# An attention and gating kernel whose vector work is dealt out anew over the engines, and whose head and batch ends are ordered anew

## The chip, the cores and the metric

The kernel runs on one core of a Trainium2 chip. The metric is the device time of one execution in microseconds (us). The engines are PE (matmul), DVE (vector), ACT (scalar functions), POOL and SP; each works through its own instructions in order. PE writes to PSUM, from where DVE and ACT read; POOL reads and writes SBUF alone. POOL and SP also issue DMAs, in the order of their other instructions.

## The reference

Four batches of q, k and v, each 6336 x 256. For each batch a 256 x 256 attention matrix over the channels is made from column-normed q and k; v times this matrix is x, and a gate with two 256 x 256 weights follows.

```python
qn = q / (np.linalg.norm(q, axis=1, keepdims=True) + 1e-06)
kn = k / (np.linalg.norm(k, axis=1, keepdims=True) + 1e-06)
s = kn.transpose(0, 2, 1) @ qn / tau
a = softmax(s)                       # over the last axis
x = (v @ a).reshape(25344, 256)
H = np.maximum(x @ w_h, 0.0)
T = 1.0 / (1.0 + np.exp(-(x @ w_t + b_t)))
out = T * H + (1.0 - T) * x
```

## The kernel before

**Tiles.** A batch is 49 tiles of 128 rows and a tail of 64. Tiles come in six chunks (8, 8, 8, 8, 8, 9 tiles); q, k and v are loaded chunk by chunk with a cast to f16 (`load_chunk`, L74), all by DMAs that POOL issues. There are 9 chunk buffers each for q and k, 7 for v. The output leaves by chunks too, in three buffers, by DMAs that SP issues (L392).

**Gram work.** `stage1(b, i)` (L160 to L162) is one gram unit: for one tile of q and k six matmuls add k'q, k'k and q'q into `sg` (two PSUM banks). A batch has 50 units (49 tiles and the tail).

**Chain.** `chain(b)` makes the batch's matrix from `sg` in five steps. `norms` takes the diagonals on DVE (L181), the square root on ACT (L191), and 1/norm on DVE; `bcast` spreads the column factors by a matmul with ones (L212) into PSUM; `soft` multiplies on DVE (L220), takes Exp on ACT (L226) and scales on DVE (L240) into `mr`; `trans` transposes `mr` on PE (L255) with a copy on DVE (L257); `fold` multiplies it with both gate weights (L265), and the copies to f16 (L272 on ACT, L273 on DVE) complete `mr` = [a, a w_h, a w_t].

**Slots.** A batch has 25 slots (`npair`), each two tiles of v. Slot i of batch b issues, in this order: `main(b, i)`, with four matmuls of 512 columns into `xh` = [x, x w_h] (L324; two buffers of two banks) and, into `tt` (one bank), the bias b_t by a matmul of 512 columns (L331) and x w_t (L335); then `pending`, the last slot's `finish`; then `elementwise(b, i)`; then `transposes` of the v tiles two slots ahead (L303 into `vtps`, one PSUM bank, copied by DVE in L306); then `issue_loads`, which issues the loads whose buffers are free by then; then, while there is a next batch, two or three of its gram units, 50 over 18 slots, and after them one step of its chain per slot.

**Elementwise.** With hh = relu(x w_h) on ACT (L351), uu = 1 - T by a Sigmoid with scale -1 on ACT (L354) and dd = hh - x on DVE (L359), the product dd = uu * dd runs on POOL (L367). `finish` writes o = hh - dd on DVE (L384) and, at the end of a chunk, its store.

**Order.** The order is written out by hand: each engine takes its instructions in the order in which this code issues them. Before the slots all of batch 0's gram units, its loads, its chain and two `transposes` are issued. A buffer that is used again waits for its last reader.

## Time and profile before

| | us |
|---|---|
| median of three runs | 379.46 (378.46 to 380.11) |
| profiled execution | 382.07 |
| span of the profiled execution, first to last instruction | 380.3 |
| PE busy in it | 294.3 (77%) |
| DVE, ACT, POOL busy | 186.9, 147.3, 170.7 |
| chain of waits that ended last, by engine | PE 46%, DMA 17%, DVE 13%, POOL 12% of the span |

The profile is of one execution, 0.7% above the median. Its shares are means over stages that differ, so the stretches in the next section but one are read one by one: loads and gram of batch 0, the slots of batches 0 to 2 with the next batch's gram units in the first 18 and its chain in the last 7, and batch 3 without gram work. "Idle before, releaser" in a row is how long the engine stood idle before that instruction and whose end let it go.

### The profile page before, as it was taken

The numbers are of one execution on the slowest core, as the hardware profiler recorded it, in microseconds if no ns is written. First come the engines' busy times: TensorE is split into PE (matmuls) and PEld (weight loads), VectorE is DVE, ScalarE is ACT, GpSimd is POOL, SyncE is SP. The second block draws the span as 40 slices with busy tenths as digits, with TensorE's granted clock in tenths as the row PEclk, the third lists the DMA queues.
The fourth block names the chain that finished last, engine by engine and source line by source line (L and its number), as shares of the span: only waits on it lengthen the run. The fifth ranks groups of instructions, "written<-read, shape, count | busy, mean of one in ns | idle before, by whom it ended". The sixth has DMA issues, their size and how long they took to land.

```text
span 380.3 us, 6361 instructions
## 1 busy us (share of the span) xinstructions
PE 294.3 (77%) x2540; PEld 204.1 (54%) x2540; DVE 186.9 (49%) x394; ACT 147.3 (39%) x251; POOL 170.7 (45%) x189
## 2 busy tenths in 40 slices
PE   0937639089999679999996889999977876767650
PEld 0836516067777445777774457777744444434320
DVE  0000132056555757556557566555665765656551
ACT  1000033114333674344336753344466644444430
POOL 6242212355466525654665254444442545444441
PEclk9997967779999989999999799999998999999995
DMA  7999999999999993999999925566335032222113
GB/s 138 209 162 214 210 214 214 214 213 268 258 242 248 266 266 66 259 240 210 215 237 231 243 41 175 162 167 165 69 110 164 0 133 110 110 112 97 49 77 132
DMA packets 15821, 65.68 MB, mean 173 GB/s; under 512 B 1712, under 2 KB 3504, under 8 KB 12720
## 3 DMA queue, kind: packets, MB, share of 16 engines
q0 software_dynamic: 12016, 39.33, 55.1%
q1 hardware_dynamic: 3776, 25.95, 16.8%
q8 instruction: 20, 0.33, 0.3%
q14 instruction: 9, 0.07, 0.1%
HBM read 78.64 MB, written 25.95 MB: 275 GB/s over the span
## 4 chain that ended last, share of the span: by engine, by line
PE 46%; DMA 17%; DVE 13%; POOL 12%; ACT 5%; issue 4%; POOLq 0%; DVEq 0%; ACTq 0%
PE xh L324 15%; POOL dd L367 11%; DMA k<-in_k_dram 9%; PE sg L160 8%; PE t L335 7%; DVE dd L359 6%; DVE o L384 5%; DMA v<-in_v_dram 5%; PE sg L162 4%; PE sg L161 4%; PE vtps L303 4%; PE t L331 3%; DMA q<-in_q_dram 3%; ACT L354 2%; ACT hh L351 2%
## 5 line engine op out<-in xcount | busy, mean ns | idle before, releaser
L367 POOL TENSOR_TENSOR dd<-uu,dd 128x512 f32<-128x512 f32 (+1 forms) x104 | 127.1, 1224 | 149.9 <-DVE dd L359 114.3
L384 DVE TENSOR_TENSOR o<-hh,dd 128x512 f32<-128x512 f32 (+1 forms) x100 | 70.1, 701 | 113.8 <-POOL dd L367 113.8
L351 ACT ACTIVATE hh<-xh 128x512 f32<-128x512 f32 (+1 forms) x104 | 59.8, 579 | 153.5 <-PE xh L324 151.6
L160 PE MATMUL sg<-q,k 128*128 128x256 f16 x392 | 93.9, 281 | 19.8 <-DMA k<-in_k_dram 19.8
L324 PE MATMUL xh<-mr,vtsb 128*128 128x512 f16 (+1 forms) x400 | 108.0, 393 | 0.5 <-DVE vtsb L306 0.5
L161 PE MATMUL sg<-k 128*128 128x128 f16 x392 | 87.9, 224 | 0.0
L162 PE MATMUL sg<-q 128*128 128x128 f16 x392 | 87.8, 224 | 0.0
L359 DVE TENSOR_TENSOR dd<-hh,xh 128x512 f32<-128x512 f32 (+1 forms) x104 | 68.5, 662 | 12.3 <-ACT hh L351 11.2
L303 PE MATMUL vtps<-ident,v 128*128 128x128 f16 x392 | 39.4, 224 | 32.5 <-DVE vtsb L306 32.5
L354 ACT ACTIVATE uu<-t 128x512 f32<-128x512 f32 (+1 forms) x104 | 59.9, 580 | 10.4 <-PE t L335 4.6
L335 PE MATMUL t<-mr,vtsb 128*128 128x256 f16 (+1 forms) x400 | 62.3, 279 | 0.0
L335 PEld LDWEIGHTS <-vtsb 128*128 128x128 f16 (+1 forms) x400 | 39.4, 100 | 29.4 <-issue 5.5
L303 PEld LDWEIGHTS <-v 128*128 128x128 f16 x392 | 31.3, 100 | 40.6 <-issue 38.3
L324 PEld LDWEIGHTS <-vtsb 128*128 128x128 f16 (+1 forms) x400 | 35.9, 101 | 28.9 <-issue 5.0
L160 PEld LDWEIGHTS <-k 128*128 128x128 f16 x392 | 39.5, 101 | 20.3 <-DMA k<-in_k_dram 20.3
L162 PEld LDWEIGHTS <-q 128*128 128x128 f16 x392 | 39.5, 101 | 5.6
L306 DVE COPY vtsb<-vtps 128x512 f16<-128x512 f16 (+1 forms) x104 | 41.7, 404 | 1.7 <-PE vtps L303 1.6
L161 PEld LDWEIGHTS <-k 128*128 128x128 f16 x392 | 39.5, 101 | 0.0
L331 PE MATMUL t<-btb,ident 128*128 128x512 f16 x100 | 39.0, 390 | 0.6 <-ACT uu L354 0.6
L181 DVE SCALAR_TENSOR_TENSOR junk<-sg,ident 128x128 f32<-128x128 f32 x16 | 4.6, 289 | 42.9 <-PE sg L162 42.5
L74 POOL DMA_DIRECT2D q<-in_q_dram x24 | 13.1, 546 | 16.8 <-DMA k<-in_k_dram 8.5
L74 POOL DMA_DIRECT2D k<-in_k_dram x24 | 13.0, 544 | 16.5 <-DMA v<-in_v_dram 8.6
(49 smaller groups left out, 100.0 us busy)
## 6 DMA issues: line engine op xcount, KB each, us to landing
out_dram<-o SPq DMA_DIRECT2D x20, 1024.0 KB, 7.0
q<-in_q_dram POOLq DMA_DIRECT2D x20, 512.0 KB, 14.0
k<-in_k_dram POOLq DMA_DIRECT2D x20, 512.0 KB, 15.8
v<-in_v_dram POOLq DMA_DIRECT2D x20, 512.0 KB, 10.3
out_dram<-o SPq DMA_DIRECT2D x4, 1152.0 KB, 5.5
q<-in_q_dram POOLq DMA_DIRECT2D x4, 576.0 KB, 14.7
k<-in_k_dram POOLq DMA_DIRECT2D x4, 576.0 KB, 16.1
v<-in_v_dram POOLq DMA_DIRECT2D x4, 576.0 KB, 7.7
```

Of the source, the lines that this page charges most:

```text
L160: nc.tensor.matmul(sg[:, c, 0:C], ka[:, cs], qa, start=first, stop=False)
L161: nc.tensor.matmul(sg[:, c, C : C + P], ka[:, cs], ka[:, cs], start=False, stop=False)
L162: nc.tensor.matmul(sg[:, c, C + P : C + 2 * P], qa[:, cs], qa[:, cs], start=False, stop=last)
L303: nc.tensor.transpose(ps[:, u, c, 0:nr], src[:, bass.ts(c, P)], ident[0:nr, 0:nr])
L324: nc.tensor.matmul(xh[0:nr, u, :], vt[:, u, kt, 0:nr], mr[:, kt, 0 : 2 * C], start=(kt == 0), stop=(kt == 1),)
L331: nc.tensor.matmul(tt, ident, btb, start=True, stop=False)
L335: nc.tensor.matmul(tt[0:nr, u, :], vt[:, u, kt, 0:nr], mr[:, kt, 2 * C : 3 * C], start=False, stop=(kt == 1 and u == 0),)
L351: nc.scalar.activation(out=hh[0:nr, us, :], in_=xh[0:nr, us, C : 2 * C], func=Act.Relu)
L354: nc.scalar.activation(out=uu[0:nr, us, :], in_=tt[0:nr, us, :], func=Act.Sigmoid, scale=-1.0)
L359: nc.vector.tensor_tensor(out=dd[0:nr, us, :], in0=hh[0:nr, us, :], in1=xh[0:nr, us, 0:C], op=AluOp.subtract,)
L367: nc.gpsimd.tensor_tensor(out=dd[0:nr, us, :], in0=uu[0:nr, us, :], in1=dd[0:nr, us, :], op=AluOp.mult)
L384: nc.vector.tensor_tensor(out=ot, in0=hh[0:nr, us, :], in1=dd[0:nr, us, :], op=AluOp.subtract)
```

## The change

- POOL keeps the loads alone in batches 0 to 2: the product moves to DVE. In batch 3 (`end`) odd slots keep it on POOL and even ones run it on DVE. DVE's order in a slot becomes dd(i), then `finish` of slot i-1, then the product of slot i.
- The gate in batches 0 to 2 is a Tanh: with t = tanh(-z/2), the product is (t + 1) * dd and o = hh - 0.5 * that product, each one scalar_tensor_tensor on DVE. Batch 3 keeps Sigmoid.
- The copy of the transposed v moves from DVE to ACT.
- The norms take the square root by an integer start value and three Newton rounds on DVE instead of ACT's Sqrt: 13 more instructions of 128x4.
- The chain's transposes use the PSUM buffer of `vtps` and the fold one of `xh` instead of `sg`'s, so gram units of the next batch may stand between the chain's steps. In batch 0's head 11 units of batch 1 do (5, 3 and 3); the other 39 are spread over 18 slots.
- In batch 3 the last chunk is stored pair by pair. `issue_loads(HEAD)` bounds the first round of loads at 40 entries; that round ends at 21 in both kernels.

```diff
-            nrm = small.tile([P, 4], f32, tag="nrm", name=f"nrm{b}")
-            nc.scalar.activation(out=nrm, in_=x, func=Act.Sqrt)
+            nc.vector.tensor_scalar(
+                out=x, in0=x, scalar1=1e-30, scalar2=None, op0=AluOp.max, op1=AluOp.bypass
+            )
...
+            for _ in range(3):
+                nc.vector.scalar_tensor_tensor(
+                    out=w, in0=y, scalar=-0.5, in1=y, op0=AluOp.mult, op1=AluOp.mult
+                )
+                nc.vector.tensor_tensor(out=w, in0=w, in1=x, op=AluOp.mult)
+                nc.vector.scalar_tensor_tensor(
+                    out=y, in0=w, scalar=1.5, in1=y, op0=AluOp.add, op1=AluOp.mult
+                )
...
-            atps = psum.tile([P, 2, 2, P], f16, tag="sg", bufs=1, name=f"atps{b}")
+            atps = psum.tile([P, 2, 2, P], f16, tag="vt", bufs=1, name=f"atps{b}")
...
-            ah = psum.tile([P, 2, 2 * C], f32, tag="sg", bufs=1, name=f"ah{b}")
+            ah = psum.tile([P, 2, 2 * C], f32, tag="xh", bufs=2, name=f"ah{b}")
...
-            nc.vector.tensor_copy(
-                out=vt[:, u0 : u0 + nu, :, 0:nr], in_=ps[:, u0 : u0 + nu, :, 0:nr]
-            )
+            nc.scalar.copy(out=vt[:, u0 : u0 + nu, :, 0:nr], in_=ps[:, u0 : u0 + nu, :, 0:nr])
...
+                func=Act.Sigmoid if end else Act.Tanh,
+                scale=-1.0 if end else -0.5,
...
-            nc.gpsimd.tensor_tensor(
-                out=dd[0:nr, us, :], in0=uu[0:nr, us, :], in1=dd[0:nr, us, :], op=AluOp.mult
-            )
+        if before_product is not None:
+            before_product()
+        for us, nr in sp:
+            if end:
+                eng = nc.gpsimd if i % 2 else nc.vector
+                eng.tensor_tensor(
+                    out=dd[0:nr, us, :], in0=uu[0:nr, us, :], in1=dd[0:nr, us, :], op=AluOp.mult
+                )
+            else:
+                nc.vector.scalar_tensor_tensor(
+                    out=dd[0:nr, us, :],
+                    in0=uu[0:nr, us, :],
+                    scalar=1.0,
+                    in1=dd[0:nr, us, :],
+                    op0=AluOp.add,
+                    op1=AluOp.mult,
+                )
...
+                elif end and j == NJ - 1:
+                    nc.sync.dma_start(out=dst[:, s : s + nu, :], in_=ot)
...
-    issue_loads()
-    for step in chain(0):
-        step()
+    issue_loads(HEAD)
+    norms, bcast, soft, trans, fold = chain(0)
+    norms()
+    bcast()
+    soft()
     for i in range(LOOK):
         transposes(0, i)
...
+    head(5)
+    trans()
+    head(3)
+    fold()
+    head(3)
...
-            if pending is not None:
-                pending()
-            pending = elementwise(b, i, xh, tt)
+            pending = elementwise(b, i, xh, tt, pending)
...
-                want = min(S + 1, -(-(S + 1) * (i + 1) // S1_SLOTS))
+                want = min(S + 1, base - (base - S - 1) * (i + 1) // S1_SLOTS)
```

How this moves instructions is shown at three places. In the names below the digits behind a tile's name are batch and chunk (loads, o) or batch and slot (dd, uu, hh, vtsb); the number after the last underscore is a count of the program.

The first place is the start of batch 0's slots, on POOL, in the kernel before:

```order
L74 DMA v1_0_454<-in_v_dram 128x2048
L74 DMA q2_0_456<-in_q_dram 128x2048
L74 DMA k2_0_458<-in_k_dram 128x2048
L367 TENSOR_TENSOR dd0_0_532<-uu0_0_531,dd0_0_532 128x512
L367 TENSOR_TENSOR dd0_1_578<-uu0_1_577,dd0_1_578 128x512
L367 TENSOR_TENSOR dd0_2_622<-uu0_2_621,dd0_2_622 128x512
L74 DMA v1_1_634<-in_v_dram 128x2048
```

There a product stood behind 21 loads of the first round and ahead of the next three; POOL now has, at the same place:

```order
L75 DMA v1_0_454<-in_v_dram 128x2048
L75 DMA q2_0_456<-in_q_dram 128x2048
L75 DMA k2_0_458<-in_k_dram 128x2048
L75 DMA v1_1_707<-in_v_dram 128x2048
L75 DMA q2_1_709<-in_q_dram 128x2048
```

Now load follows on load, and no product stands among them. ACT's first instructions, before:

```order
L191 ACT_TABLE_LOAD
L191 ACTIVATE nrm0_466<-nrm20_461 128x4
L214 COPY cqbs0_476<-cqb0_474 128x256
L226 ACT_TABLE_LOAD
L226 ACTIVATE e0_481,rs0_482<-t10_478,inv0_468 128x256 x2
L272 CAST mr0_488<-ah0_498 128x512
L351 ACTIVATE hh0_0_530<-xh0_0_519 128x512
L354 ACT_TABLE_LOAD
L354 ACTIVATE uu0_0_531<-t0_0_520 128x512
```

and now:

```order
L244 ACT_TABLE_LOAD
L244 COPY cqbs0_489<-cqb0_487 128x256
L256 ACTIVATE e0_494,rs0_495<-t10_491,inv0_480 128x256 x2
L336 COPY vtsb0_0_509<-vtps0_0_504 128x512
L336 COPY vtsb0_1_516<-vtps0_1_511 128x512
L302 CAST mr0_501<-ah0_574 128x512
L383 ACTIVATE hh0_0_610<-xh0_0_599 128x512
L385 ACTIVATE uu0_0_611<-t0_0_600 128x512
```

The Sqrt and two of the three table loads are gone here, and the copies of v stand behind e; in the whole program ACT had 15 table loads and has two, the other one ahead of batch 3's first Sigmoid.

The second place is where the chain of batch 2 begins on DVE, behind batch 1's last gram slot, before:

```order
L384 TENSOR_TENSOR o1_4_2344<-hh1_17_2346,dd1_17_2348 128x512
L359 TENSOR_TENSOR dd1_18_2386<-hh1_18_2384,xh1_18_2372 128x512
L306 COPY vtsb1_20_2396<-vtps1_20_2391 128x512
L181 SCALAR_TENSOR_TENSOR junk2_2404,nrm22_2405<-sg2_1596,ident0_76 128x128 x4
L193 TENSOR_SCALAR inv2_2412<-nrm2_2410 128x4
L196 RECIPROCAL inv2_2412<-inv2_2412 128x4
L200 TENSOR_SCALAR dcat2_2415<-ident0_76,inv2_2412 128x128 x2
L384 TENSOR_TENSOR o1_4_2344<-hh1_18_2384,dd1_18_2386 128x512
```

and now (the three Newton rounds are three instructions each, of which the first round is shown):

```order
L392 TENSOR_TENSOR dd1_18_2411<-hh1_18_2409,xh1_18_2398 128x512
L429 SCALAR_TENSOR_TENSOR o1_4_2376<-dd1_17_2372,hh1_17_2370 128x512
L407 SCALAR_TENSOR_TENSOR dd1_18_2411<-uu1_18_2410,dd1_18_2411 128x512
L182 SCALAR_TENSOR_TENSOR junk2_2430,nrm22_2431<-sg2_1622,ident0_76 128x128 x4
L192 TENSOR_SCALAR nrm22_2431<-nrm22_2431 128x4
L197 TENSOR_SCALAR y2_2437<-nrm22_2431 128x4
L205 TENSOR_SCALAR y2_2437<-y2_2437 128x4
L214 SCALAR_TENSOR_TENSOR w2_2438<-y2_2437 128x4
L217 TENSOR_TENSOR w2_2438<-w2_2438,nrm22_2431 128x4
L218 SCALAR_TENSOR_TENSOR y2_2437<-w2_2438,y2_2437 128x4
```

The product of slot 18 stands ahead of the norms, and 15 instructions of 128x4 stand where two stood.

The third place is batch 3 on DVE, before:

```order
L384 TENSOR_TENSOR o3_0_3681<-hh3_2_3709,dd3_2_3711 128x512
L359 TENSOR_TENSOR dd3_3_3737<-hh3_3_3735,xh3_3_3723 128x512
L306 COPY vtsb3_5_3747<-vtps3_5_3742 128x512
L384 TENSOR_TENSOR o3_0_3681<-hh3_3_3735,dd3_3_3737 128x512
L359 TENSOR_TENSOR dd3_4_3764<-hh3_4_3762,xh3_4_3749 128x512
```

and now:

```order
L392 TENSOR_TENSOR dd3_3_3788<-hh3_3_3786,xh3_3_3775 128x512
L429 SCALAR_TENSOR_TENSOR o3_0_3739<-dd3_2_3762,hh3_2_3760 128x512
L392 TENSOR_TENSOR dd3_4_3814<-hh3_4_3812,xh3_4_3801 128x512
L429 SCALAR_TENSOR_TENSOR o3_0_3739<-dd3_3_3788,hh3_3_3786 128x512
L403 TENSOR_TENSOR dd3_4_3814<-uu3_4_3813,dd3_4_3814 128x512
```

dd of a slot now stands ahead of o of the slot before it, and the product of slot 4 is DVE's own; that of slot 3 is POOL's.

## Rows read from the trace of the kernel before

**Rows 1.** Stretches: us, busy us of PE, PEld, DVE, ACT, POOL, PEclk, DMA share, GB/s.

```profile
45.92:57.97 12.05, 4.04 (x18) 1.99 (x19) 5.17 (x21) 3.54 (x8) 2.64 (x5) 0.70 1.06 212
57.97:147.21 89.24, 73.93 (x637) 51.63 (x636) 44.47 (x93) 37.83 (x63) 41.29 (x46) 0.91 1.01 233
147.21:201.85 54.64, 53.75 (x538) 40.80 (x535) 32.31 (x59) 22.04 (x38) 32.07 (x36) 1.00 0.99 216
201.85:224.43 22.58, 18.15 (x103) 9.69 (x102) 14.30 (x39) 15.24 (x27) 9.40 (x10) 0.85 0.79 195
224.43:301.02 76.59, 70.63 (x639) 49.97 (x637) 46.78 (x98) 36.88 (x64) 34.97 (x33) 0.98 0.47 128
301.02:366.02 65.00, 45.53 (x311) 26.10 (x309) 39.52 (x75) 29.05 (x50) 30.15 (x26) 1.00 0.25 101
366.02:380.30 14.28, 2.14 (x9) 0.60 (x9) 3.96 (x8) 1.44 (x5) 3.81 (x4) 0.69 0.22 88
```

**Rows 2.** Timeline of POOL: start us, us, engine line op out<-in xcount [idle before <-releaser].

```profile
74.05 0.53 POOL L74 DMA_DIRECT2D k<-in_k_dram  x1 [1.68 <-DMA v<-in_v_dram]
74.60 1.27 POOL L367 TENSOR_TENSOR dd<-uu,dd 128x512 f32<-128x512 f32 x1
...
363.18 1.27 POOL L367 TENSOR_TENSOR dd<-uu,dd 128x512 f32<-128x512 f32 x1 [1.47 <-DVE dd L359]
```

**Rows 3.** Timeline of DVE, head, first stall, a tail, batch 3 and the end.

```profile
52.40 0.61 DVE L240 TENSOR_SCALAR mr<-e,ri 128x256 f16<-128x256 f32 x2
...
75.91 0.69 DVE L384 TENSOR_TENSOR o<-hh,dd 128x512 f32<-128x512 f32 x1 [14.11 <-POOL dd L367]
...
203.60 0.69 DVE L359 TENSOR_TENSOR dd<-hh,xh 128x512 f32<-128x512 f32 x1
...
206.10 0.17 DVE L193 TENSOR_SCALAR inv<-nrm 128x4 f32<-128x4 f32 x1 [0.27 <-ACT nrm L191]
206.31 0.18 DVE L196 RECIPROCAL inv<-inv 128x4 f32<-128x4 f32 x1
...
361.74 0.69 DVE L384 TENSOR_TENSOR o<-hh,dd 128x512 f32<-128x512 f32 x1 [1.11 <-POOL dd L367]
362.35 0.68 DVE L359 TENSOR_TENSOR dd<-hh,xh 128x512 f32<-128x512 f32 x1
...
372.71 0.41 DVE L384 TENSOR_TENSOR ot<-hh,dd 64x256 f32<-64x256 f32 x1
```

**Rows 4.** Timeline of PE, three gram slots' xh and a tail's broadcast.

```profile
172.33 1.03 PE L324 MATMUL xh<-mr,vtsb 128*128 128x512 f16 x4
...
174.95 1.03 PE L324 MATMUL xh<-mr,vtsb 128*128 128x512 f16 x4
...
178.02 1.03 PE L324 MATMUL xh<-mr,vtsb 128*128 128x512 f16 x4
...
208.52 1.22 PE L212 MATMUL cqb<-dcat,ones 128*128 128x256 f32 x2 [3.02 <-ACT uu L354]
```

**Rows 5.** Groups by line: shapes xcount | busy us, mean ns | idle us <-releasers.

```profile
L384 DVE TENSOR_TENSOR o<-hh,dd 128x512 f32<-128x512 f32 x96 | 66.4, 692 | 112.0 <-POOL dd L367 112.0
L351 ACT ACTIVATE hh<-xh 128x512 f32<-128x512 f32 x96 | 57.2, 596 | 150.6 <-PE xh L324 148.7 <-ACT uu L354 1.9
L306 DVE COPY vtsb<-vtps 128x512 f16<-128x512 f16 x96 | 40.0, 417 | 1.7 <-PE vtps L303 1.6
L226 ACT ACT_TABLE_LOAD x4 | 5.1, 1283 | 0.1
L181 DVE SCALAR_TENSOR_TENSOR junk<-sg,ident 128x128 f32<-128x128 f32 x16 | 4.6, 289 | 42.9 <-PE sg L162 42.5
L384 DVE TENSOR_TENSOR o<-hh,dd 128x256 f32<-128x256 f32 x4 | 3.7, 933 | 1.7 <-POOL dd L367 1.7
L272 ACT CAST mr<-ah 128x512 f16<-128x512 f32 x4 | 2.3, 586 | 5.7 <-PE ah L265 5.7
```

**Rows 6.** DMA view of 66.68 to 66.73: KB, us from issue to landing.

```profile
k<-in_k_dram POOLq DMA_DIRECT2D x1, 576.0 KB, 20.3
```

More of the change, by code (lines that the diff above doesn't have):

```diff
@@ L20 @@
 LOOK = 2
+HEAD = 40
 @with_exitstack
@@ L129, in mark, with issue_loads @@
         done_use[(kind, b * NJ + j)] = clock[0]
-    def issue_loads():
-        while ptr[0] < len(seq):
+    def issue_loads(most=99):
+        while ptr[0] < min(len(seq), most):
             kind, b, j = seq[ptr[0]]
@@ L342, in main, with elementwise @@
         return xh, tt
-    def elementwise(b, i, xh, tt):
+    def elementwise(b, i, xh, tt, before_product):
+        end = b == B - 1
         hh = small.tile([P, 2, C], f32, tag="hh", bufs=4, name=f"hh{b}_{i}")
@@ L383, in finish @@
                     ot = otail[0:nr, :, :]
-                nc.vector.tensor_tensor(
-                    out=ot, in0=hh[0:nr, us, :], in1=dd[0:nr, us, :], op=AluOp.subtract
+                nc.vector.scalar_tensor_tensor(
+                    out=ot,
+                    in0=dd[0:nr, us, :],
+                    scalar=-1.0 if end else -0.5,
+                    in1=hh[0:nr, us, :],
+                    op0=AluOp.mult,
+                    op1=AluOp.add,
                 )
@@ L403, with head @@
     clock[0] += 1
-    issue_loads()
-    for step in chain(0):
-        step()
+    issue_loads(HEAD)
[3 more added lines that the diff above has]
+    soft()
     for i in range(LOOK):
         transposes(0, i)
+    s1_head = 0
+    def head(n):
+        nonlocal s1_head
+        for _ in range(n):
+            stage1(1, s1_head)
+            s1_head += 1
+    head(5)
[3 more added lines that the diff above has]
+    head(3)
     pending = None
```

39 lines of the change are left out of this document (28 added, 11 removed).

## The prediction

> **What bounds the kernel now.** I read the table of stretches first [rows 1], cut at the first xh matmul of each batch: batch 0 runs from 57.97 to 147.21 us (89.24), batch 1 to 224.43 (77.22), batch 2 to 301.02 (76.59), the 24 slots of batch 3 before its last to 366.02 (65.00), and 14.28 us are left. Three limits alternate. In the stretch of batch 1 that carries gram units (147.21 to 201.85) PE is busy 53.75 of 54.64 us at full clock: PE is the bound, and only fewer columns would help. In the rest of that batch (201.85 to 224.43: 7 slots and the softmax chain) PE is busy 18.15 of 22.58, at a granted clock of 0.85. In batch 3 PE is busy 45.53 of 65.00 and no engine is full, so a loop of waits sets the pace.
>
> That loop shows in the timelines of POOL and DVE: product 363.18 to 364.45 on POOL [rows 2], o(i-1) at 361.74, and dd(i) right behind it at 362.35 on DVE [rows 3]. dd(i) stands behind o(i-1), which waits for POOL's product (1.11 us idle in that row), and the next product waits for dd(i): 1.27 + 0.69 + 0.68 and hand-overs are 2.7 us a slot, and 65.00 / 24 = 2.71. In batch 0 there is a single stall as well: DVE's first o starts at 75.91 after 14.11 us of waiting for POOL [rows 3], and POOL starts the first product at 74.60, right behind the load k issued at 74.05 [rows 2]: 21 loads stand ahead of it, and they issue only as older ones land.
>
> PE's cost of a slot comes from three xh starts in gram slots, 2.62 and 3.07 us apart [rows 4], with two and three gram units: 0.44 a unit, 1.74 without. Check: 18 x 1.74 + 50 x 0.44 = 53.3 against 54.64; the rest is one wait in the batch's first slot.
>
> **The change, part by part.**
> *Product to DVE, copy to ACT.* DVE then does dd, o and product in a slot. Neighbours start 0.61 apart (361.74, 362.35) [rows 3], so 3 x 0.61 = 1.8 us. The new scalar_tensor_tensor from SBUF isn't in the trace. Its nearest rows are the tensor_tensor on the same operands, 692 ns, and one scalar_tensor_tensor of 128 columns, 289 ns [rows 5]. They agree if both pay 1 column per 1.05 ns: 289 + 384 x 1.05 = 692. I take 0.61 of spacing, bounds 0.55 and 0.70. ACT gets a copy beside hh and uu (596 each): between 417 (the copy on DVE) and 586 (ACT's cast of as many columns out of PSUM) [rows 5]; I take 586, so about 1.75 a slot. Both are under a gram slot's 2.7 to 3.0, so there they are hidden behind PE, with 1.1 us of cover. Without gram they are level with PE's 1.74. tanh is taken at the sigmoid's price, one function pass each.
>
> *Batch 0's stall goes.* POOL has no product, so nothing is behind the loads. What would be late next is the supply of k for batch 1: its last chunk, issued at 66.70, lands 20.3 us later, at 87.0 [rows 6]. Unit 40 needs it in slot 13; with the times below, at 62.1 + 13 x 2.7 + 1.7 = 98.9. That is 12 us of slack, less what two earlier stores take from it (about 5 us). So the cover holds, and the cost is 0 (bounds 0 and 6).
>
> *Head.* The chain's Newton steps put 13 more 128x4 instructions on DVE. Two such instructions start 0.21 apart (206.10, 206.31), so +2.7, and the square root's 0.27 of waiting goes [rows 3]; 0.5 of an Exp table load (1283 ns) [rows 5] that delayed e goes too, since the loads of tables are two in all and the first stands at the start. mr is thus ready about 1.9 later, at 54.9 instead of 53.0 (52.40 + 0.61) [rows 3]. The eleven gram units cost 0.44 each at full clock. PE's granted clock was 0.70 of full over 45.92 to 57.97, a mix of its two levels [rows 1]; so I charge the first five with 3.9 us, the rest at 0.44. The two copies of v wait on ACT behind e, so the units begin at about 54.5: units to 58.4, transposes and three units 1.6, the fold 0.9, three units 1.3, and batch 0 starts at 62.1 (bounds 59.5 and 64).
>
> *Gram slots.* Batch 0 has 39 units left: 18 x 1.74 + 39 x 0.44 = 48.5. Batches 1 and 2 keep 50: 53.4 each. For them this part of the change brings 1 us, the wait named above.
>
> *Tail of a batch.* Now the norms start behind dd, o and product of slot 18. From the end of gram: 1.75 until hh is there (201.85 to DVE's dd at 203.60, the same path) [rows 3], three DVE operations 1.8, norms 1.3 + 15 x 0.21 + dcat 0.4 = 4.85. The broadcast matmul starts at 8.5, against 208.52 - 201.85 = 6.67 before, where it waited for a uu behind table loads [rows 4]. From it to the next batch before took 224.43 - 208.52 = 15.9. In program order, the product ahead of the softmax pieces adds 0.6, the Exp load ahead of e takes 0.7 net with it, the chain's transposes now share v's PSUM buffer and wait for one ACT copy more (0.8), and the last three slots run at DVE's 2.3 instead of the loop's 2.7 (-1.1): 15.5. So the tail is 24.0 against 22.6: 1.4 worse, not better (bounds 21 and 26.5). Batch 0: 48.5 + 24.0 = 72.5. Batches 1, 2: 53.4 + 24.0 = 77.4 each.
>
> *Batch 3.* Even products run on DVE, odd ones on POOL; dd(i) no longer stands behind o(i-1). PE would allow 1.74 a slot. But two instructions with both inputs in SBUF meet: while POOL runs product i, DVE runs o(i-1). The trace has that meeting four times, in the last slot of each batch: o of 128x256, begun while POOL multiplies the second piece, takes 933 ns [rows 5], where the 64x256 one, of as many columns, takes 0.41 us with POOL idle [rows 3]: DVE lost 0.52 us. Here o(i-1) starts first: back to back with dd(i) it would start at 362.35 + 0.61 = 362.96, POOL's product started at 363.18 [rows 2, 3]. No row shows who waits then. If POOL waits out the o, the loop over two slots is o 0.6, product 1.27, hand-overs 0.3, then o, product and dd 0.6 + 0.6 + 0.7 = 4.0, or 1.97 a slot: 24 x 1.97 = 47.3. dd(i+1) fits beside POOL, since xh lies in PSUM. Without any blocking the loop is 1.27 + 0.3 + 3 x 0.6 = 3.4, under PE's 3.5, and it is 24 x 1.75 = 42.0. If POOL goes first and DVE waits, as in those four meetings, it is 1.4 and then five passes of 0.6, 4.4 a pair and 52.8. I take 47.3, and 1.0 for the one Sigmoid table load in slot 0 (1283 ns): 48.3.
> The Trainium skill, page "SBUF — State Buffer", section "Who interferes with whom", says that a DVE operation with two SBUF inputs and a GpSimd one that reads SBUF exclude each other, and that the one that starts first holds the port for its whole length. By that rule the sum is the 47.3 above; by the four rows alone it would be 52.8. The four rows agree with the rule, since POOL was first in each.
>
> *End.* Before, the last slot's xh to the last o took 366.02 to 373.12 (372.71 + 0.41), 7.1, then 7.2 to the span's end. The last product moves from POOL (1.27 and hand-overs 0.3) to a DVE pass of 0.6, 1.0 less, and dd no longer stands behind an o that waits 1.1 to 1.4 for POOL: 4.7. The last chunk's store is cut in five, so the end waits for a small one: 5.5 (bounds 3.5 and 7.2). 10.2 against 14.3.
>
> **Sum** in the profiled execution (span 380.30): 62.1 + 72.5 + 77.4 + 77.4 + 48.3 + 10.2 = 347.9, that is 32.4 less. The profiled execution took 382.07, the median of the three runs is 379.46, 0.7% lower; I subtract the 32.4 from the median: **347 us**.
>
> **Rivals.**
> *No blocking in batch 3.* For it: POOL's product and DVE's o may interleave if DVE is first. Against it: the four 933 ns. 347 - 5.3 = 342.
> *POOL holds DVE up in batch 3.* For it: the same four rows. Against it: o starts earlier. 347 + 5.5 = 352.5.
> *The tail is longer,* since DVE is the in-order owner of norms, products and softmax pieces, and each of its waits (for e, for hh at half clock) delays all: 26.5 instead of 24.0 in three batches, 354.5. For it: DVE's sum in the tail is 12.8 + 4.85 + 4, about the whole tail.
> *Supply.* With batch 0 14 us earlier, k's last chunks are late after all: up to 6, 353.
> *Slower.* One mechanism: the 72 chunk loads that POOL issues hold up DVE's two-SBUF passes, of which there are now two a slot instead of one. A load's issue takes 0.53 [rows 2], three per four slots: 0.4 a slot. A gram slot has 1.1 of cover, so it decides only from 1.1 + 32.4 / 54 = 1.7 us a slot, four times that; then 380 and more. Against it: the 96 o's, in a run with the same loads, mean 692 ns, like the o at 361.74 [rows 3, 5].
> That the change doesn't do what it says (products or table loads left in place) is ruled out by the instruction order shown above.
>
> **How the numbers follow.** Forecast 0.42; no blocking 0.20; POOL first 0.17; long tail 0.12; supply 0.07; slower 0.02. All rivals but the last lie at 342 to 354.5; the bounds of head, end and tail add some 5 us to either side of them, so 336 to 359 leaves out under 2 in 10. About 0.5% can be told from no change in this kernel; by the cases above faster 0.97, within 0.01, slower 0.02.
>
> **What would show it.** Right: no DVE wait for POOL over 2 us in batch 0; main(0,0) near 62 and main(1,0) near 135; xh starts in gram slots still 2.62 and 3.07 apart; tails of 24; xh in batch 3 near 2.0 apart, alternating; two table loads. Wrong: k waits on PE after 62 us; a batch 3 slot at 1.75 or above 2.2; DVE passes of more than 0.7 us in gram slots; a tail under 21 or over 27.

## The result and the profile after

The changed kernel takes **347.12 us** (median of four runs, 346.81 to 348.55) against 379.78 (378.46 to 382.06) in the same session: a ratio of 0.914, 95% interval 0.909 to 0.919. The prediction was 347. The profiled execution of after took 346.81 with a span of 344.8; that of before had 380.3. The spans thus differ by 35.5 us where 32.4 had been predicted, and the medians by 32.7, because the profiled execution of before lay 0.7% above its median while that of after is the lowest of its four.

The stretches of after, cut as [rows 1] at the first xh of each batch (columns: us; busy us of PE, PEld, DVE, ACT, POOL; granted clock; DMA share; GB/s). The second to fourth rows are batch 0, then batch 1 cut where its gram units end:

```profile
45.92:62.42 16.50, 9.58 (x85) 7.88 (x85) 6.76 (x33) 3.10 (x8) 3.72 (x7) 0.69 1.06 213
62.42:135.05 72.63, 65.11 (x572) 45.38 (x570) 51.78 (x106) 42.53 (x81) 12.21 (x23) 0.98 1.05 249
135.05:188.64 53.59, 53.59 (x537) 40.81 (x535) 35.02 (x59) 31.01 (x57) 7.00 (x14) 1.00 1.05 253
188.64:212.61 23.97, 16.86 (x103) 9.54 (x102) 18.98 (x54) 12.48 (x28) 1.51 (x3) 0.86 0.82 207
212.61:290.16 77.55, 70.92 (x638) 50.51 (x636) 53.99 (x112) 43.59 (x84) 2.65 (x5) 0.96 0.43 120
290.16:333.67 43.51, 42.51 (x312) 26.44 (x310) 36.85 (x62) 41.07 (x75) 17.31 (x11) 1.00 0.36 144
333.67:344.80 11.13, 2.12 (x11) 0.58 (x8) 5.17 (x11) 2.08 (x6) 1.74 (x2) 0.70 0.37 138
```

| us | before | predicted | after |
|---|---|---|---|
| start of batch 0 | 57.97 | 62.1 | 62.42 |
| batch 0 | 89.24 | 72.5 | 72.63 |
| batch 1 (gram slots + tail) | 77.22 | 77.4 (53.4 + 24.0) | 77.56 (53.59 + 23.97) |
| batch 2 | 76.59 | 77.4 | 77.55 |
| batch 3, 24 slots | 65.00 | 48.3 | 43.51 |
| end | 14.28 | 10.2 | 11.13 |
| span | 380.3 | 347.9 | 344.8 |

Of the seven stretches one is far off, batch 3, by 4.8 us; the end is off by 0.9 and the others by at most 0.3. In the gram slots of batch 1 PE is busy all 53.59 us: the bound of before is still there, now without a wait. All of the gain is in batch 0 (the stall), batch 3 and the end. The head is 4.5 us longer and batch 1's tail (a batch's last seven slots, with the chain) 1.4, as the sum had it.

Batch 3 in the timelines of DVE, then of POOL (start us, us, engine, line, operation, out<-in, idle before and its releaser; the rows of before are in [rows 2, 3]; here and below, rows of other instructions in between can be left out):

```profile
305.81 0.68 DVE L392 TENSOR_TENSOR dd<-hh,xh 128x512 f32<-128x512 f32 x1
306.41 0.69 DVE L429 SCALAR_TENSOR_TENSOR o<-dd,hh 128x512 f32<-128x512 f32 x1
307.01 0.68 DVE L392 TENSOR_TENSOR dd<-hh,xh 128x512 f32<-128x512 f32 x1
308.26 0.69 DVE L429 SCALAR_TENSOR_TENSOR o<-dd,hh 128x512 f32<-128x512 f32 x1 [0.57 <-POOL dd L403]
308.87 0.68 DVE L403 TENSOR_TENSOR dd<-uu,dd 128x512 f32<-128x512 f32 x1
309.47 0.68 DVE L392 TENSOR_TENSOR dd<-hh,xh 128x512 f32<-128x512 f32 x1
```

```profile
306.64 1.59 POOL L403 TENSOR_TENSOR dd<-uu,dd 128x512 f32<-128x512 f32 x1 [2.07 <-DVE dd L392]
310.30 1.59 POOL L403 TENSOR_TENSOR dd<-uu,dd 128x512 f32<-128x512 f32 x1 [2.07 <-DVE dd L392]
```

Here is the loop over two slots, 305.81 to 309.47, 3.66 us. DVE's o(i-1) runs from 306.41; POOL's product starts at 306.64, in the middle of it, and its record is 1.59 us where [rows 2] has 1.27: it was held up 0.32 us, and o was not (0.69, as before). The dd from 307.01, which reads one input from PSUM, runs its 0.68 us beside POOL's product. o(i) starts 0.03 us after the product's end, the next product 0.61 and the next dd 0.60 later.

The groups by shape of after (count | busy us, mean ns | idle us and releasers) that answer [rows 5]:

```profile
L429 DVE SCALAR_TENSOR_TENSOR o<-dd,hh 128x512 f32<-128x512 f32 x96 | 65.7, 685 | 5.9 <-POOL dd L403 5.8
L403 POOL TENSOR_TENSOR dd<-uu,dd 128x512 f32<-128x512 f32 x12 | 19.1, 1588 | 52.3 <-DVE dd L392 48.2 <-ACT hh L383 2.1 <-ACT vtsb L336 2.1
L407 DVE SCALAR_TENSOR_TENSOR dd<-uu,dd 128x512 f32<-128x512 f32 x72 | 49.2, 684 | 0.1
L336 ACT COPY vtsb<-vtps 128x512 f16<-128x512 f16 x96 | 55.6, 579 | 0.7 <-PE vtps L333 0.7
L385 ACT ACT_TABLE_LOAD x1 | 1.3, 1283 | 0.1
```

DVE's wait for POOL has shrunk from 112.0 us [rows 5] to 5.8. The scalar_tensor_tensor of two SBUF inputs costs 684 ns (692 had been taken), the copy on ACT 579 (586 taken). There are two table loads in all, this one in batch 3's first slot and one before the head's first ACT instruction, where there were 15.

The tail of batch 1, whose gram units end at 188.64, in the timeline of PE:

```profile
197.15 1.19 PE L242 MATMUL cqb<-dcat,ones 128*128 128x256 f32 x2 [4.86 <-DVE dcat L230]
198.14 1.91 PE L352 MATMUL xh<-mr,vtsb 128*128 128x512 f16 x4
201.55 1.03 PE L352 MATMUL xh<-mr,vtsb 128*128 128x512 f16 x4
205.70 0.38 PE L285 MATMUL atps<-ident,mr 128*128 128x128 f16 x4 [2.25 <-ACT vtsb L336]
```

The broadcast matmul stands at 188.64 + 8.51; 8.5 had been predicted. PE waits 4.86 us for the norms, has its next xh at half clock (1.91 us instead of 1.03 for the four matmuls), and waits 2.25 us more ahead of the chain's transposes.

### The profile page after: what moved, and what is told of

It reads as the page before. It is cut to its first block, busy times and chain, and to the rows that moved or that the text cites. A ratio compares the mean times of both kernels' runs of the same rounds, so it can differ in the third digit from the quotient of the medians.

```text
span 344.8 us, 6497 instructions
## 1 busy us (share of the span) xinstructions
PE 287.4 (83%) x2540; PEld 204.9 (59%) x2540; DVE 209.0 (61%) x434; ACT 177.2 (51%) x338; POOL 62.6 (18%) x97
## 4 chain that ended last, share of the span: by engine, by line
PE 63%; DVE 11%; DMA 11%; issue 5%; POOL 4%; ACT 3%; POOLq 1%; DVEq 0%; ACTq 0%
PE xh L352 20%; PE sg L161 11%; PE t L363 9%; DMA k<-in_k_dram 7%; PE sg L162 5%; PE sg L163 5%; PE vtps L333 5%; PE t L359 5%; DMA btb<-in_moe_b_t_dram 4%; POOL dd L403 4%; DVE dd L392 3%; DVE dd L403 2%; ACT hh L383 1%; PE cqb L242 1%; DVE junk L182 1%
## 5 line engine op out<-in xcount | busy, mean ns | idle before, releaser
L161 PE MATMUL sg<-q,k 128*128 128x256 f16 x392 | 95.0, 283 | 19.2 <-DMA k<-in_k_dram 19.2
L352 PE MATMUL xh<-mr,vtsb 128*128 128x512 f16 (+1 forms) x400 | 106.3, 388 | 0.1
L429 DVE SCALAR_TENSOR_TENSOR o<-dd,hh 128x512 f32<-128x512 f32 (+1 forms) x100 | 67.4, 674 | 5.9 <-POOL dd L403 5.8
L363 PE MATMUL t<-mr,vtsb 128*128 128x256 f16 (+1 forms) x400 | 61.6, 276 | 0.0
L336 ACT COPY vtsb<-vtps 128x512 f16<-128x512 f16 (+1 forms) x104 | 57.7, 560 | 0.7 <-PE vtps L333 0.7
L407 DVE SCALAR_TENSOR_TENSOR dd<-uu,dd 128x512 f32<-128x512 f32 (+1 forms) x78 | 51.5, 663 | 0.1
L75 POOL DMA_DIRECT2D v<-in_v_dram x24 | 12.8, 532 | 156.9 <-PE vtps L333 129.1
L244 ACT COPY cqbs<-cqb 128x256 f32<-128x256 f32 x4 | 1.5, 372 | 65.4 <-PE cqb L242 65.4
```

The lines of the kernel that those rows point to most:

```text
L161: nc.tensor.matmul(sg[:, c, 0:C], ka[:, cs], qa, start=first, stop=False)
L336: nc.scalar.copy(out=vt[:, u0 : u0 + nu, :, 0:nr], in_=ps[:, u0 : u0 + nu, :, 0:nr])
L352: nc.tensor.matmul(xh[0:nr, u, :], vt[:, u, kt, 0:nr], mr[:, kt, 0 : 2 * C], start=(kt == 0), stop=(kt == 1),)
L363: nc.tensor.matmul(tt[0:nr, u, :], vt[:, u, kt, 0:nr], mr[:, kt, 2 * C : 3 * C], start=False, stop=(kt == 1 and u == 0),)
L429: nc.vector.scalar_tensor_tensor(out=ot, in0=dd[0:nr, us, :], scalar=-1.0 if end else -0.5, in1=hh[0:nr, us, :], op0=AluOp.mult, op1=AluOp ...
```

## The experiments

**Batch 3: who waits for whom.** This is the term that was far off, and the step on which the prediction had bet without a row. Three kernels change what runs beside what there. First, all its products on POOL:

```diff
-                eng = nc.gpsimd if i % 2 else nc.vector
+                eng = nc.gpsimd
```

> The changed kernel with all products of batch 3 on POOL instead of every second one. My theory (POOL waits for DVE's o to end, 0.55 us, and then takes its own 1.27): every slot is 1.27 + 0.55 + 0.03 = 1.85 us, 24 slots 44.4 against 43.5 after, and the last slot ends 1 us later; 347.5 to 349 us, POOL's product records 1.55 to 1.85 us in every slot. Rival without any exclusion: POOL's record is 1.27, a slot is PE's 1.74, 24 slots 41.8, and the time is at most 346.5 us. Rival that POOL's start first would stretch o: records of o over 0.9 us and slots over 2.1 us, 354 us and more.

Measured: 353.1 us (ratio 0.929, 0.923 to 0.936), 6 us over after; 24 slots of 48.33 us and an end of 13.3. That is far from my theory and near the last rival (o over 0.9 us, 354 us), but the o that grows is only every second one: from the ninth slot on, slots take 1.74 and 2.37 us by turns, 2.05 on average. The timelines of DVE and of POOL show why:

```profile
313.86 0.68 DVE L392 TENSOR_TENSOR dd<-hh,xh 128x512 f32<-128x512 f32 x1
315.10 1.75 DVE L429 SCALAR_TENSOR_TENSOR o<-dd,hh 128x512 f32<-128x512 f32 x1 [0.56 <-POOL dd L403]
316.76 0.67 DVE L392 TENSOR_TENSOR dd<-hh,xh 128x512 f32<-128x512 f32 x1
317.36 0.68 DVE L429 SCALAR_TENSOR_TENSOR o<-dd,hh 128x512 f32<-128x512 f32 x1
```

```profile
313.48 2.81 POOL L403 TENSOR_TENSOR dd<-uu,dd 128x512 f32<-128x512 f32 x2 [1.29 <-ACT uu L385]
317.58 2.81 POOL L403 TENSOR_TENSOR dd<-uu,dd 128x512 f32<-128x512 f32 x2 [1.29 <-ACT uu L385]
```

POOL runs two products back to back (x2, 2.81 us; by their single records 1.59 and 1.27, so the first is held up and the second is not). The second starts at 315.02, as soon as the first is through, since its dd is ready, and so 0.08 us ahead of the o that the first one releases: that o takes 1.75 us instead of 0.68. The side that is held up changes with every slot. My error was to take one side for the whole stretch.

Second, all products of batch 3 on DVE, so that the two engines never meet (`eng = nc.vector`):

> The changed kernel with all products of batch 3 on DVE, so that no two engines meet with two SBUF inputs. My theory: a slot is three DVE passes 0.605 apart, 1.82 us, 24 slots 43.6, the same as the 43.5 of the changed kernel; the time is 347 us give or take 1, and POOL's share of batch 3 was worth nothing (0.55 of waiting for the port eats what it takes off DVE). Every o is 0.68 us. Rival: POOL's help is worth what it takes off DVE, half a pass a slot, 0.3 x 24 = 7 us; then it is 354 us.

Measured: 344.5 us (0.906, 0.901 to 0.912; after 0.909 to 0.919). The stretches of its 24 slots and of its end (columns as in [rows 1]):

```profile
291.89:335.14 43.25, 42.28 (x311) 26.42 (x309) 42.37 (x74) 41.30 (x75) 0.00 (x0) 1.00 0.36 147
335.14:344.50 9.36, 2.12 (x9) 0.58 (x8) 5.55 (x12) 1.89 (x5) 0.00 (x0) 0.72 0.42 153
```

The 24 slots take 43.25 us against 43.51, as the theory had it: POOL's half of the products was worth nothing in batch 3. The rival (354) falls. The two intervals overlap, so the times alone don't tell this kernel from after; the trace does, in the end: 9.36 us instead of 11.13, which I had not expected. Only 0.3 of that is DVE's (the last o ends 5.55 us behind the last slot's first xh, in after 5.87). The other 1.5 come from POOL's closing DRAIN, the wait that POOL stands in at the end of the program: in after it lasts from 335.88 to 344.02, 6.54 us past the end of POOL's last product, though the last store has landed at 341.57. Here POOL has no product, that DRAIN is over by 276, and the span ends 0.9 us behind the last store's landing. One tail of this execution is 1.5 us longer than those of after, and the granted clock falls to the lower of PE's two levels a second time there.

Third, a copy that nobody reads, to let POOL start ahead of o in odd slots:

```diff
+        if end and i % 2:
+            fill = small.tile([P, C], f32, tag="fill", name=f"fill{b}_{i}")
+            nc.vector.tensor_copy(out=fill, in_=xh[:, 0, 0:C])
         if before_product is not None:
             before_product()
```

> The changed kernel with one added DVE copy (128x256 out of PSUM, into a buffer that nobody reads) between dd of slot i and o of slot i-1 in the odd slots of batch 3, so that POOL's product starts ahead of o. My theory (whichever starts first keeps the other out for its whole length): POOL's product records fall back to 1.27 us, the o behind it stretches from 0.68 to 1.3 us or more, and a pair of slots is copy 0.35, the wait for POOL of 1.0, then five passes of 0.6: 4.4 us instead of 3.66, so 24 slots take 52.8 and the time is 356 us. Rival (DVE always goes ahead of POOL): o keeps 0.68, POOL's record grows beyond 1.59, a pair is 3.66 plus the copy's 0.3, 351 us. Rival (no exclusion): neither record stretches and the copy hides beside POOL, 347 us.

Measured: 354.2 us (0.930, 0.926 to 0.934), a pair of slots 4.36 us (4.4 expected), 24 slots 51.57. DVE in its timeline, then POOL's row there and its group by shape:

```profile
316.32 0.68 DVE L392 TENSOR_TENSOR dd<-hh,xh 128x512 f32<-128x512 f32 x1
316.92 0.41 DVE L400 COPY fill<-xh 128x256 f32<-128x256 f32 x1
317.25 1.71 DVE L432 SCALAR_TENSOR_TENSOR o<-dd,hh 128x512 f32<-128x512 f32 x1
```

```profile
317.14 1.27 POOL L406 TENSOR_TENSOR dd<-uu,dd 128x512 f32<-128x512 f32 x1 [3.09 <-DVE dd L392]
```

```profile
L406 POOL TENSOR_TENSOR dd<-uu,dd 128x512 f32<-128x512 f32 x12 | 15.2, 1267 | 63.6 <-DVE dd L392 57.4 <-ACT hh L383 6.2
```

POOL now starts at 317.14, 0.11 us ahead of o, and keeps 1267 ns on average over all twelve odd slots; o pays 1.0 us more. The rivals (DVE always first, no exclusion) fall. In after POOL paid, here DVE, and apart from the copy itself only the order of the two starts was changed: the start decides, and the second waits until the first is nearly through. How long it is held follows from how far the two records overlap: 0.46 us of overlap cost 0.32 in after, 1.16 cost 1.02 here, in both 0.14 less. The Trainium skill states this ("SBUF — State Buffer", section "Who interferes with whom": a DVE instruction with two SBUF inputs contends with a GpSimd instruction that reads SBUF, the lock on the shared ports is exclusive, and the order of issue decides who blocks); 1588 against 1267 ns on POOL and 1.71 against 0.69 us on DVE agree with it, each way round.

**The two main parts, each alone on the kernel before.** The product on DVE in all slots (one word at L367, `nc.vector`), in the old order:

> The kernel before with one part of the change alone: the product runs on DVE in every slot; order of the passes, sigmoid and its table loads, copies on DVE, square root and head stay. My theory: POOL then has nothing behind the loads, so the 14.1 us wait of DVE's first o in batch 0 goes (about -13, since the first slots' lost buffers are caught up). In batch 3 a slot is then four DVE passes, dd, product and o at 0.61 and the copy of v at 0.42, 2.2 us instead of 2.71, so 24 slots take 53 instead of 65 (-12). The tails have the same four passes in place of the 2.7 us loop, about -1 each. The sum is some 353.5 us, a ratio near 0.93. Rival: the gain hangs on the new order, the missing table loads and the copy on ACT; then this kernel stays at 365 us or above. Second rival: two-SBUF products on DVE beside POOL's load issues get slower; then the 128x512 passes show over 0.75 us and the stall of batch 0 stays in part.

Measured: 361.1 us (0.945, 0.939 to 0.952). Its profiled execution is the lowest of four, 3.8 us below the median, so the stretches tell of places more than of the sum. Batch 0 took 77.08 us (12.2 less, 13 expected), so the stall is POOL's loads ahead of its first product. Batch 3 took 55.51 instead of the 53 expected: 2.33 us a slot. And batches 1 and 2 became 0.8 and 1.0 longer instead of a microsecond shorter each. Two rows of batch 3, DVE and PE, for the first miss:

```profile
323.91 0.42 DVE L306 COPY vtsb<-vtps 128x512 f16<-128x512 f16 x1
324.38 0.38 PE L303 MATMUL vtps<-ident,v 128*128 128x128 f16 x4 [0.43 <-DVE vtsb L306]
```

The copy stands behind the product in DVE's order, PE's transposes wait for it (one PSUM buffer), and the next xh stands behind them: the passes don't run back to back, since DVE's own copy closes a loop through PE and ACT. In the tails of batches 1 and 2, 1.3 and 1.5 us longer than before, PE waits 3.45 us ahead of `cqb` for a uu behind a table load (before 3.02 [rows 4]). So the loop that the product had left did not bound the tail; which other step of the chain made it longer by the remaining microsecond isn't shown.

The order alone: o(i-1) behind dd(i), the product still on POOL.

```diff
-            if pending is not None:
-                pending()
-            pending = elementwise(b, i, xh, tt)
+            pending = elementwise(b, i, xh, tt, pending)
...
+        if before_product is not None:
+            before_product()
```

> The kernel before with another part alone: o of slot i-1 is issued behind dd of slot i instead of ahead of it; the product stays on POOL, and so do the table loads and copies. My theory: the stall of batch 0 stays in full (POOL's first product still stands behind the loads it issues; DVE waits some 14 us for POOL), so batch 0 is 87 to 90 us. In batch 3 the loop of waits is cut: a slot is one product of POOL, 1.27, plus the wait for o to end, 0.55, and 0.03, 1.85 us instead of 2.71, so 24 slots take 44.4 instead of 65 (-20.6), and the last slots of the tails go faster by 2 to 3 us a batch. The sum is some 352.5 us. Together with the other single change the two gains (26 and 27 us) are more than the whole change's 32.7: they overlap in batch 3. Rival: the loop is not the order but POOL's own time; then a slot of batch 3 stays near 2.7 us and the time above 372 us.

Measured: 359.3 us (0.942, 0.938 to 0.947). Batch 0 took 89.58 (87 to 90 expected): the stall stayed. Batch 3 took 45.40 us (44.4 expected): 1.86 us a slot, all of them POOL's:

```profile
316.65 1.66 POOL L369 TENSOR_TENSOR dd<-uu,dd 128x512 f32<-128x512 f32 x1 [0.19 <-DVE dd L359]
318.50 1.67 POOL L369 TENSOR_TENSOR dd<-uu,dd 128x512 f32<-128x512 f32 x1 [0.20 <-DVE dd L359]
```

As in the kernel with all products of batch 3 on POOL, POOL does every product here, yet it waits for dd each time (0.2 us), so DVE's o always has the start and POOL always pays 0.4: 1.86 us a slot against 2.05 there. Batches 1 and 2 took 1.2 and 2.1 us less, of which 1.1 each in the tails, less than the 2 to 3 expected; the other 1.0 of batch 2 is the wait in its first gram slots, which is gone there. Each part alone takes some 24 us off the span (24.8 and 24.3; by the medians 19.9 and 21.8), both and all the rest 35.5 (32.7). So the parts don't add. They overlap in batch 3, where either one breaks the loop of 2.71 us; only the product cures batch 0.

**The smaller parts, undone one at a time on the kernel after.** The copy of v back on DVE (`nc.vector.tensor_copy` at L336):

> The changed kernel with the copies of the transposed v on DVE again. My theory: nothing changes in gram slots (DVE's 2.2 us a slot is under PE's 2.62 to 3.07), a tail grows by 2 us (five or six copies of 0.42), and in batch 3 a pair of slots grows by two copies, at least 0.42 each of which part may hide beside POOL's product: 1.9 to 2.2 us a slot, 24 slots 46 to 53. The time is 355 to 362 us. Rival: the copies hide in DVE's waits: 347 to 349 us.

Measured: 369.0 us (0.969, 0.963 to 0.975), far beyond what I expected: 22 us over after. Batch 3 took 51.3 (within the bounds), but the tails 28.1, 28.2 and 29.4 instead of 24. PE in such a tail:

```profile
214.41 0.58 PE L285 MATMUL atps<-ident,mr 128*128 128x128 f16 x4 [4.26 <-DVE vtsb L336]
214.79 1.91 PE L352 MATMUL xh<-mr,vtsb 128*128 128x512 f16 x4
```

With products, norms and softmax pieces on DVE the copy's place in its order is late, PE stands behind it for 4.26 us (2.25 in after), and the next xh runs at half clock once more. So the change needs the copy on ACT, though the copy's own time is longer there (579 ns; 417 on DVE [rows 5]).

The sigmoid in all four batches:

> The changed kernel with the sigmoid in all four batches instead of the tanh in three. My theory: two table loads of 1.28 us come back in each of the three tails (Exp, then Sigmoid again), one of them on the chain from the norms to mr, and the one in batch 3's first slot is already paid; tails 25 to 25.5 instead of 24.0, and the time is 350.5 us. Rival: ACT's queue hides them all; 347 us, tails 24. Rival: both stand on the chain and hold up hh of the last slots too: tails 27, 356 us.

Measured: 356.1 us (0.936, 0.930 to 0.942), 9 over after, near the last rival; tails 27.4, 27.7, 26.1. ACT in the tail of batch 1:

```profile
206.20 1.28 ACT L256 ACT_TABLE_LOAD   x1
207.50 0.51 ACT L256 ACTIVATE e<-t,inv 128x256 f32<-128x256 f32 x1
209.09 1.28 ACT L385 ACT_TABLE_LOAD   x1
210.88 0.58 ACT L336 COPY vtsb<-vtps 128x512 f16<-128x512 f16 x1
```

One load delays e, the other the copy of v for which PE waits: both stand on the chain. The last tail is 2.1 us longer than in after; the first two are 3.5 and 3.7 longer, since there the longer wait (4.26 us ahead of the transposes in this tail, 2.25 in after) is followed by a second stretch at half clock. That Exp and Tanh need no load between them, while Exp and Sigmoid do, agrees with the Trainium skill ("ScalarE: Activation LUTs", section "Table sets: the hidden batching unit").

ACT's square root in place of the Newton steps:

```diff
-            for _ in range(3):
-                nc.vector.scalar_tensor_tensor(
-                    out=w, in0=y, scalar=-0.5, in1=y, op0=AluOp.mult, op1=AluOp.mult
-                )
...
+            nc.scalar.activation(out=nrm, in_=x, func=Act.Sqrt)
```

> The changed kernel with ACT's square root in place of the 13 small Newton steps on DVE. My theory: the Newton steps cost 13 x 0.20 = 2.6 us of each tail, and ACT's root costs 0.3 of hand-overs and 1.3 of a table load ahead of it, so each tail gains some 0.9, the head 1, in all 344 us. Rival: with the root the loads of tables come back (root, Exp, Tanh: two or three loads of 1.28 us for each batch on an ACT that has 1.75 of work in a 1.74 us slot), each delays the chain or a hh behind it; then the tails are 1 to 3 us longer each and the time is 349 to 354 us. Told apart by the length of the tails (24.0 after) and the count of table loads.

Measured: 341.7 us (0.897, 0.891 to 0.903), 5.4 under after: tails 23.0 (23.1 expected), batch 0 starts 1.2 earlier. There are nine table loads again. ACT at the end of batch 1's gram units (186.60):

```profile
189.48 1.28 ACT L193 ACT_TABLE_LOAD   x1
191.49 0.21 ACT L193 ACTIVATE nrm<-nrm 128x4 f32<-128x4 f32 x1 [0.73 <-DVE junk L182]
191.60 0.58 ACT L355 ACTIVATE hh<-xh 128x512 f32<-128x512 f32 x1
192.20 1.28 ACT L357 ACT_TABLE_LOAD   x1
```

The first load ends 0.73 us before the root's input is there and costs nothing; the second, for uu, serves the Exp too. It has a price: `dcat` is done at 192.63, 6.0 behind the last gram unit (8.3 in after), but PE's `cqb` stands at 194.15, since it takes the PSUM bank `t` that this uu still reads (3.89 us <- ACT uu in its row). So the root saves 2.3 us of the chain and the load gives 1.3 back. The Newton steps were thus a part of the change that cost time.

The head without its eleven gram units:

> The changed kernel without the eleven gram units of the next batch that stand between the steps of the first softmax chain; they fall into the slots of batch 0, which has 50 units there again. My theory: eleven units cost 4.9 us at full clock in batch 0 (48.7 to 53.6), and in the head they took 3.9 at half clock and 2.6 at full clock but partly hid the chain's waits (trans for mr, fold for at, main for the casts, about 4 us in all), so main(0,0) starts at 59.5 to 60 instead of 62.4 and the time rises by some 2.5 us, to 349.5. Rival: the units hide nothing, since the first chain's end is set by mr; then main(0,0) starts at 57.5 and the time stays within 1 us of 347. Second rival: without them PE stays at half clock into batch 0, and the time rises by 4 us or more.

Measured: 350.7 us (0.924, 0.919 to 0.930), where 349.5 was expected. main(0,0) starts at 58.90, 3.5 us earlier, but batch 0's gram slots take 56.37 us instead of 48.7 with eleven units more, which are worth 4.9. The two stretches of this kernel's first slot, then the head's first units in after:

```profile
58.90:61.90 3.00, 2.86 (x8) 1.12 (x8) 0.84 (x2) 0.60 (x1) 0.82 (x2) 0.50 1.06 213
61.90:64.74 2.84, 2.84 (x25) 2.48 (x23) 1.22 (x2) 1.07 (x2) 0.53 (x1) 0.57 1.04 209
54.49:58.20 3.71, 3.71 (x28) 3.18 (x28) 0.53 (x2) 0.59 (x1) 0.94 (x2) 0.50 1.06 213
```

The number behind the five counted busy times is the granted clock: 0.50 and 0.57 of full. The first slot takes 5.84 us, 2.8 more than one at full clock (3.06). In after, the head's units ran at half clock instead (54.87 to 58.2), and the first slot at full clock. So the gram slots of batch 0 end 4.1 us later (3.5 less, 4.9 and 2.8 more); 1.5 more are a second stretch at half clock in batch 1's tail, as in the kernel with all products on DVE. The theory lacked the clock, which only the second rival had; by the medians the time rose 3.6 us.

Two parts of the change were not undone by themselves: the chain's PSUM buffers and the stores of batch 3 pair by pair.

**The tail, moved forward.** After the change the tails are 24 us with PE busy 16.9. Norms right behind the last gram unit:

```diff
                     if steps is None:
                         steps = chain(b + 1)
-                    elif steps:
+                        steps.pop(0)()
+                    elif i >= S1_SLOTS + 1 and steps:
                         steps.pop(0)()
```

> The changed kernel with one move: the norms are issued right behind the batch's last gram unit, in slot 17, instead of behind dd, o and the product of slot 18; the other four steps of the chain stay at their slots. My theory: PE's 4.86 us of waiting for dcat in each tail is the path, and DVE reaches the norms 3.4 us earlier, so tails are 20.6 us instead of 24.0 and the time is 337 us. Rival: DVE's sum in the tail (seven slots of 1.82 and 8 us of chain, 20.7) or a clock that falls later instead is the bound behind it, and the tails stay at 22 to 23: 341 to 344 us. Rival: the hh and uu of slot 18 wait behind the norms in DVE's order and give all of it back: 347 us.

Measured: 341.0 us (0.899, 0.894 to 0.904). PE's wait for dcat fell from 4.86 to 2.03 us, and two tails took 20.8 us, near the theory's 20.6; that of batch 1 took 22.4, with a second stretch at half clock after its wait ahead of the transposes; and batch 0 began 1.2 us later than in after, where the head's code is the same: PE's granted clock rose at 60.5 there, not at 58.2. So the mechanism held and the sum was 4 us short; the granted clock accounts for 2.8 of it, by its later rise in the head and by the second fall in one tail, of which the first rival had the latter.

Early norms, the square root, all products of batch 3 on DVE and the tanh form there as well:

> The early norms, ACT's square root, all products on DVE in batch 3 and the tanh form there too (one table load less), joined on the changed kernel. My theory: the gains add where they lie in different stretches: early norms -3.4 and the root -0.9 in each tail, -1.2 in the head, -1.1 in batch 3's first slot for the load, -1.7 at the end: 344.8 - 16.9 = 328 us of span, a time of 330 us. Rival: the root's gain lies on the same wait as the early norms (PE's wait for dcat, 4.86 us, which the early norms alone bring to 1.5), so only part of it is left, and the table load delays e: tails 21 to 22 and 334 us.

Measured: 333.0 us (0.878, 0.873 to 0.883), between theory (330) and rival (334). Tails 20.3, 21.3 and 21.7: the rival's overlap is real. What PE waits for in this kernel (engine, line <- releaser: us in total, times, longest):

```profile
PE atps L257 <- ACT vtsb L308: 7.6, 3, 3.0
PE t L331 <- ACT uu L357: 5.8, 3, 1.9
```

The second row is the table load ahead of uu, 1.9 us a tail, which shows once the wait that hid it is gone. The first is left from after; it points at the softmax piece, which stands on DVE behind a dd that waits 1.9 us for its hh. Moved ahead of that dd:

```diff
-                    elif i >= S1_SLOTS + 1 and steps:
+                    elif i >= S1_SLOTS + 1 and i != S1_SLOTS + 2 and steps:
                         steps.pop(0)()
+                        if i == S1_SLOTS + 1:
+                            steps.pop(0)()
```

> The joined version with one step of the chain moved: the softmax piece (t1, e, ri, mr) stands right behind the broadcast in slot 19 instead of behind dd, o and the product of slot 20, and the transposes of mr and the fold stay in slots 21 and 22. My theory: in the joined version DVE waits 1.9 us for hh of slot 20 with the softmax piece behind it, and PE then waits 2.3 us for atps; with the piece in that gap mr is ready 3.7 us earlier, PE's wait goes, tails are 18.5 to 19 us instead of 20.3 to 21.7, and the time is 326 us. Rival: DVE's sum in the tail (seven slots of 1.82 and 6 us of chain, 18.7) and ACT's (seven slots of 1.75, two table loads, 3 us of chain, 17.9) leave no room, DVE waits for e with dd of slot 20 behind it, and PE waits for a free xh instead: tails 20 and more, 331 to 333 us. Rival: the granted clock falls at another place; then single tails differ by 1.5 us.

Measured: **327.3 us** (0.864, 0.859 to 0.869), the fastest of all; tails 19.2, 19.2 and 20.3. The same two waits:

```profile
PE t L331 <- ACT uu L357: 6.7, 5, 1.9
PE atps L257 <- ACT vtsb L308: 3.0, 3, 1.0
```

The tail of batch 1 as a stretch (columns as above):

```profile
182.32:201.54 19.22, 15.21 (x103) 8.55 (x102) 16.83 (x41) 14.93 (x31) 1.50 (x3) 1.00 1.05 264
```

PE's clock stays at full there (0.86 in after), and no wait of PE in it is over 1.93 us. The third tail, with waits of 1.93 and 0.80, has a stretch at half clock again and takes 1.1 more.

## Why the prediction was right, point by point

**What bounds the kernel.** Held. The stall of batch 0 was POOL's loads: the product's move alone cured it, the order alone did not. The loop of batch 3 was the order of o and dd: the order alone cut it from 2.71 to 1.86 us a slot.

**Head.** 62.1 predicted, 62.42 measured. The first five units took 3.81 us (54.87 to 58.68), 3.9 predicted; the clock rose at 58.2. What the sum did not say is what they buy: without them the half clock falls into batch 0's first slot.

**Gram slots, batch 0, supply.** Held to 0.2 us. DVE's and ACT's 1.8 us a slot hide under PE. PE never waits for k after the head (its 19.2 us of that are over by 46); k's last chunk was issued at 66.68 and landed 23.9 us later, at 90.6 (87 plus up to 5 predicted, 98.9 needed). Nothing of the rival on supply is seen.

**Tail.** 24.0 predicted, 23.9 to 24.0 in all three. The term "1.4 worse" was right for batch 1, from whose row it was made; in batches 0 and 2, whose tails were 21.8 and 21.9 us before, it was 2.0. The experiments show what can be taken out of a tail: the Newton steps (0.9), the late norms (3.1: they begin 3.6 us behind the last gram unit, 0.7 when moved), and a softmax piece behind a waiting dd. That the copy moved to ACT was costed at nothing, "hidden behind PE"; true in gram slots, but it is worth 4 us in a tail and 7.8 in batch 3, and taking tanh "at the sigmoid's price" left out what the sigmoid's table loads would cost on the fuller ACT, 2.1 to 3.7 us a tail. That the tail came out right all the same is because the sum started from the tail of before and added differences; it had no term for what either part spares.

**Batch 3.** The step that failed: 48.3 predicted, 43.51 measured. Its mechanism was right, POOL waits out the o that started first. By the time alone one would have believed otherwise: the rival of no blocking gave 42.0 and 1.0 for the table load, nearer than the forecast, and a slot near 1.75, which the prediction had listed as a sign of being wrong, came true in most slots. The records decide (1588 against 1267 ns, o unslowed), and the kernel that let POOL start first gave 4.36 us a pair, the 4.4 of the third case. Mis-sized were two things. The first is the loop of a pair: the sum used 1.97 a slot, 3.94 a pair (the terms as written down even add up to 4.07); it is 3.66, mainly because the hand-over from POOL to DVE is 0.03 and not 0.3, and the one from DVE to POOL (0.15) lies inside the wait for o. That is 12 x 0.28 = 3.4 us. The second is that I let every slot pay the loop: DVE falls behind PE's 1.74 by only 0.09 a slot, the two xh buffers absorbed that for the first 14 slots, and only the rest alternate between 1.74 and 1.92: about 1.5 more. The forecast of xh "near 2.0 apart, alternating" was wrong for the same reason. The load in the first slot cost 1.10 for 1.0.

**End.** 10.2 predicted, 11.13 measured. The last o ends 5.87 us behind the last slot's first xh, where 4.7 was predicted: o still waits for POOL twice there (0.57 and 0.50 us), a piece of loop that I had taken as gone. The 5.5 for a small store came near the 5.27 measured, but by luck: the last store lands 2.0 us behind the last o, and what the span waits for is POOL's closing DRAIN, 6.54 us past POOL's last product. In before it was the same DRAIN, over at 379.04, 6.54 us past the last product too, and not the store (377.37). With no product on POOL in batch 3 the end is 9.36.

**The sum.** The terms missed by +0.3, +0.1, +0.2, +0.2, -4.8 and +0.9. That the median came out at 347.1 is partly luck: the span fell by 35.5 where the sum had 32.4, and it is because the profiled execution of before stood 0.7% above the median from which I subtracted that the medians fell by only 32.7.

**Slower.** DVE's passes beside POOL's load issues mean 684 to 685 ns (o before: 692 [rows 5]). Nothing of that rival is seen.

## What to carry to other kernels

A loop of waits can be broken at any of its steps. So price a change that breaks one loop at two steps as a whole, stage by stage, and don't add the gains of its parts. Before dealing work to a second engine, see whether it meets the first on the same ports: here half the products on POOL were worth nothing in the slots and cost 1.8 us at the end. With all products on POOL a slot took 0.2 us less in the kernel where DVE always started first than in the one where the two took turns, though those two kernels differ in more than that. When a stage ends in a serial chain, ask of each step what stands ahead of it in its engine's order: here two steps moved, one function back on ACT, and batch 3's products on DVE with the tanh took another 20 us off the changed kernel.
